# Turning keys and receptances with eight 128-row products into one PSUM bank each in place of sixteen 64-row ones, in a fused RWKV-6 and token-mixing kernel on one Trainium2 core

## The chip, the cores and the metric

The kernel runs on one core of a Trainium2 chip. A core has five engines that run their own instruction streams and wait for each other at semaphores: TensorE (PE) for matrix products, VectorE (DVE), ScalarE (ACT), GpSimd (POOL) and SyncE (SP), which here issues nearly all DMA transfers. Products land in PSUM, an accumulator memory of eight banks of 2 KB per partition, from where VectorE or ScalarE take them to SBUF. The metric is device time in microseconds (us) of one execution; smaller is better.

## The reference, cut to what matters

Inputs are r, k, v and w of shape (4, 8, 768, 48) (batch, heads, sequence, head dimension), u (8, 48), and three matrices. First comes a linear attention with a decaying state, then a token mixer over its output:

```python
for t in range(S):                                   # S = 768
    cur = einsum('bhd,bhe->bhde', u * k[t], v[t])
    y[t] = einsum('bhd,bhde->bhe', r[t], state + cur)
    state = w[t][..., None] * state + einsum('bhd,bhe->bhde', k[t], v[t])
x = y.transpose(0, 2, 1, 3).reshape(B, S, H * D)     # H * D = 384
wq, wk = x @ w_q, x @ w_k                            # 64 columns each
mixed = einsum('bst,btd->bsd', scale * einsum('bsd,btd->bst', wq, wk), x)
out = maximum(mixed, 0) @ w_out
```

## The kernel before

The sequence of each batch is cut into three units of 256 positions (U), so there are 12 units, numbered 0 to 11. A unit is two chunks (c = 0, 1) of 128 positions (C). Within a chunk the recurrence is written as products of decayed keys and receptances, from chunk to chunk goes the state SB. After the third unit of a batch comes the token mixer of that batch.

What happens in a unit, by the names of the steps:

- `wg`, `kg`, `rg`, `vg` are loaded by SP in rings of four buffers, so that the loads can run several units ahead. `ln` takes the logarithm of w to `lw`; `k16`, `r16`, `v16` are casts to bf16, mostly on POOL (k, r, v in the profile).
- `cw` (PS<-CM,lw) sums the logarithms along the positions, in 16 products of 64 rows. ScalarE makes from it the decays `ep` and `en`.
- `kT` and `rT` (PS<-PM,k and PS<-PM,r) turn keys and receptances so that the head dimension lies on the partitions. A cast tensor has the positions of chunk 0 in partitions 0 to 63 and of chunk 1 in 64 to 127 (two per partition, side by side). A turning product takes 64 rows of one chunk as weights (64x128) and the 64x64 corner of the permutation PM as the moving operand. It is done 16 times for a tensor: four pairs of heads, two positions, two chunks.
- Both land in one buffer `kr` of two neighbouring PSUM banks (a "wide" buffer, line 464): chunk 0 in the first bank and chunk 1 in the second, keys in the first half of each bank and receptances in the second half. `turned` (lines 488 to 491) gives the view in which the evictions read it.
- `ks` copies the keys to SBUF; `qT` (receptances times keys, for the bonus u), `RT` (receptances times decay) and `KT` (keys times inverse decay) follow, on VectorE and POOL. Then `A` (PS<-RT,KT, 8 products of 48 rows) for each chunk, its masked eviction `AM`, and `ya` (PS<-VB,AM) and `yi` (PS<-SB,RT, 48 rows), which form y. `kb` turns KT back for the state, `kd` evicts it, `sn` (PS<-SB,IDU and PS<-VB,kd) forms the state and `SB` evicts it. `vp` (PS<-v,PM) sorts the values, `dps` (PS<-UB,qT) makes the bonus.
- The mixer: `X` forms the attention's output, `xt` and `XT` turn it (PS<-ID,X), `qk` projects it, `T`, `mx` (PS<-QK,TS), `fp` (PS<-wo,MX) and `os` end with the store.

All products go through the helper `mm` on line 179, so the profile tells them apart by tiles only. The order of the work is written out by hand: a step is added with what it waits for, and the table ORDER (line 82) lists all steps in the order in which they are issued; each engine gets its own steps in that order and runs them strictly one after the other. WAYS picks the engine of a step that could go to several, BANKS the PSUM banks of a buffer. At the end of the list stand WARM = 12 products of zeros (`z`, PS<-Z), which ORDER spreads over the program; the last of them, step 733, is the last product on TensorE.

The sixteen products for a tensor of the units 1 to 11 (the `long` form, with four positions per partition) are these, lines 470 to 477:

```python
for hp in range(2):
    for s in range(4):
        for c in range(2):
            rows = ds(c * 64, 64)
            x = c * 1024 + place + hp * C + (s % 2) * 64 + (s // 2) * 32
            mm(view(o, x, [[256, 2], [1, 32]]),
               src.tile[rows, ds(s * 256 + hp * 128, 128)],
               PM[rows, rows], trans=True)
```

Of the kernel before, what the change touches and what calls it, by code (L numbers as in the profile page):

```python
# [23 lines left out]
class Buf:  # L24
    def __init__(self, kind, tile=None):
        self.kind = kind
        self.tile = tile
        self.filler = None
        self.before = None
        self.bank = None  # L30


class Plan:
# [89 lines left out]
]  # L123
WAYS = (
    "PDDDAPPDDdPADPPDDEEEAAPPAdPAAPEAcEEAAPPAPPADPeDEEDAAAAAAAAPPDPDADPeAcEEDAPPAdPAAPEAEEEDA"
# [1 line left out]
    "DPPAPeAcceAAPPDPPPAPPAEEDDAEDADAAADAAAADADDA"  # L127
)
BANKS = [
# [6 lines left out]
]  # L136


WARM = 12


@with_exitstack
def kernel(
# [170 lines left out]
    def bank():  # L314
        return Buf("s")
# [66 lines left out]
    def unit(n, batch):  # L382
# [80 lines left out]

        kr = wide()

        def transposed(name, src, step, place):
            def f(e):
                o = at(kr, BF16)
                if long:
                    for hp in range(2):  # L470
                        for s in range(4):
# [6 lines that stand above are left out]
                    return  # L478
                for hp in range(NP):
                    for j in range(2):  # L480
                        for c in range(2):
                            rows = ds(c * 64, 64)
                            mm(o[:, ds(c * 1024 + place + hp * C + j * 64, 64)],
                               src.tile[rows, ds(j * 512 + hp * 128, 128)],
                               PM[rows, rows], trans=True)
            return add((name, n), "E", f, [step], kr, [src], mode=1)

        def turned(place, cs=(0, 1), runs=False):

            return view(at(kr, BF16), place + cs[0] * 1024, [[1024, len(cs)]] * (len(cs) > 1) +  # L490
                        ([[32, 16], [1, 32]] if runs else [[1, 512]]))

        def plain(t, cs=(0, 1), run=0):
# [172 lines left out]
        def of(c, h):  # L666
            return at(ys[c])[:, ds(h * D if end else h % 2 * 512 + (c * NP + h // 2) * D, D)]

        def f_yi(e, c, start):
            heads = [(hp, hh) for hp in range(NP) for hh in range(2)]  # L670
            if end:
                heads.sort(key=lambda x: x[1])
            for x, (hp, hh) in enumerate(heads):
                if end and x == NP:
                    nc.tensor.drain()
                mm(of(c, 2 * hp + hh), RT.tile[ds(hh * 64, D), ds((c * NP + hp) * C, C)],
                   olds[c].tile[ds(hh * 64, D), ds(hp * D, D)],
                   start=(start and hp == 0 and not (end and hh)), stop=False)

        def f_ya(e, c, start):  # L680
            for h in range(H):
                hp, hh = divmod(h, 2)
                mm(of(c, h), AM[c].tile[:, ds(hh * 512 + hp * C, C)],
# [1 line left out]

        def y_add(c):
            yas[c] = add(("ya", n, c), "E",
                         lambda e, c=c, x=ys[c].filler is None: f_ya(e, c, x), [AMs[c], VBs], ys[c],
                         [AM[c], VB])
        for c in range(2):  # L690
            if olds[c] is None:
                y_add(c)
            else:
                yis[c] = add(("yi", n, c), "E",
                             lambda e, c=c, x=ys[c].filler is None: f_yi(e, c, x),
                             [RTs[c], oldss[c]], ys[c], [RT, olds[c]], mode=1)
        for c in range(2):
            if c not in yas:
# [92 lines left out]
        def f_T(e, gs):  # L791
            for gi in gs:
                ii, c = divmod(gi, 2)
                mm(at(T)[ds(c * DH, DH), ds(0, DM)], QK.tile[:, ds(ii * QS + U + c * DH, DH)],
                   X.tile[:, ds(gi * DM, DM)], start=(gi < 2), stop=(gi >= NCH - 2))
        parts = [list(range(4)), [4], [5]] if end else [list(range(NCH))]
        Tp = [add(("T", n, gs[0]), "E", lambda e, gs=gs: f_T(e, gs),
                  [batch["k"][x] for x in gs] + [batch["x"][x] for x in gs], T, [QK, X], mode=2,
# [54 lines left out]
    for n in range(N):  # L853
        if n % NU == 0:
            batch = {"k": [], "q": [], "x": []}
        unit(n, batch)
    for x in range(WARM):
        z = bank()
        add(("z", x), "E", lambda e, z=z: mm(at(z), Z[:, ds(0, C)], Z), [], z, [z])

# [33 lines left out]
```

## Time and profile before

| | |
|---|---|
| median of 3 runs | 101.39 us (101.14 to 102.23) |
| profiled execution | 101.37 us, of which 99.6 us are the span from the first to the last instruction |
| TensorE clock granted | full over the whole span |
| keys turned (PS<-PM,k) | 192 products, 190 ns each by the record, 5.2 us of busy time |
| receptances turned (PS<-PM,r) | 192 products, 190 ns each, 4.9 us of busy time |
| full transposes of X (PS<-ID,X) | 60 products of 128x128, 220 ns each, 5.2 us |
| DMA | 24.68 MB, 248 GB/s over the span |

How to read it: a matmul's record lasts from its start to its modelled end, and several are under way at a time. So 16 products of 190 ns each can take a quarter of a us together, and what a group costs its successor is the distance between their starts. The timeline puts neighbouring instructions of one kind into a row: start, length, engine, line, operation, tiles, rows*columns of the weights, the shape that moves, and the count; in brackets stands how long the engine was idle ahead of it and what released it. "Issue" there means that nothing in the profile explains the wait.

### The profile page before, as it was taken

To read this page: it belongs to the slowest core of one execution; us is meant where nothing else is said; L and a number is where in the kernel's file an instruction comes from. 1 tells how busy PE (TensorE), PEld (TensorE's weight loads), DVE (VectorE), ACT (ScalarE), POOL (GpSimd) and SP (SyncE) were. 2 spreads that over 40 slices of the span, in tenths; PEclk is the share of its full clock that TensorE was granted. 3 is DMA by queue.
4 is the path that set the end of the run, shared out by engine and by line. 5 is a ranking of instruction groups with operands and counts; after the bars stand their busy time and mean duration, and the time that the engine had idled before them with its cause. 6 is when DMAs were issued, how large, how long until landed. Compare 5 with 4: busy or idle time off the path is not lost.

```text
span 99.6 us, 4492 instructions
## 1 busy us (share of the span) xinstructions
PE 86.6 (87%) x1906; PEld 63.3 (64%) x1911; DVE 84.9 (85%) x154; ACT 79.0 (79%) x135; POOL 69.5 (70%) x82
## 2 busy tenths in 40 slices
PE   5978796879886998999999999889998999999930
PEld 1325473756774767777776777759787687776610
DVE  6284999799979999979999999999999799783740
ACT  6034998799996799899999998999899766666920
POOL 6866354999799895799999989498996392500000
PEclk9999999999999999999999999999999999999999
DMA  1999999799999999999999977998993056030794
GB/s 17 313 327 349 324 337 296 195 295 335 289 314 298 225 311 329 344 321 268 271 330 305 316 114 218 251 156 201 282 417 115 7 210 264 10 158 7 277 367 149
DMA packets 45141, 24.68 MB, mean 248 GB/s; under 512 B 31552, under 2 KB 43968, under 8 KB 45120
## 3 DMA queue, kind: packets, MB, share of 16 engines
q1 hardware_dynamic: 44960, 24.19, 84.0%
q8 instruction: 15, 0.25, 0.9%
q10 hardware_dynamic: 160, 0.20, 0.5%
q14 instruction: 6, 0.05, 0.1%
HBM read 19.66 MB, written 4.72 MB: 245 GB/s over the span
## 4 chain that ended last, share of the span: by engine, by line
PE 37%; DVE 23%; SPq 20%; DMA 7%; issue 7%; ACT 3%; ACTq 0%; DVEq 0%
PE PS L179 37%; SPq L232 9%; SPq L237 8%; DMA vg<-in_v_dram 7%; DVE AM L595 7%; DVE X L710 6%; DVE RT L516 3%; SPq L355 2%; DVE qT L506 2%; DVE ks L333 2%; DVE SB L658 1%; ACT VB L327 1%; SPq L357 1%; ACT MX L339 1%; DVE kd L335 1%
## 5 line engine op out<-in xcount | busy, mean ns | idle before, releaser
L595 DVE TENSOR_TENSOR AM<-PS,US 128x1024 bf16<-128x1024 f32 x24 | 28.8, 1218 | 0.7 <-PE PS L179 0.7
L526 POOL TENSOR_TENSOR KT<-ks,en 128x1024 bf16<-128x1024 bf16 (+1 forms) x10 | 19.7, 1965 | 4.7 <-DVE ks L333 3.3
L575 POOL TENSOR_TENSOR Vd<-VB,dd 128x768 bf16<-128x768 bf16 (+1 forms) x14 | 18.1, 1293 | 4.5 <-ACT dd L327 3.4
L454 ACT ACTIVATE en<-PS 128x1024 bf16<-128x1024 f32 (+1 forms) x14 | 12.5, 907 | 3.0 <-PE PS L179 2.9
L179 PEld LDWEIGHTS <-KT 48*128 48x128 bf16 (+1 forms) x312 | 9.7, 94 | 6.6 <-issue 4.5
L447 ACT ACTIVATE ep<-PS 128x512 bf16<-128x512 f32 (+1 forms) x28 | 13.7, 555 | 0.1
L179 PE MATMUL PS<-wo,MX 128*128 128x384 bf16 x72 | 13.5, 327 | 0.0
L710 DVE SCALAR_TENSOR_TENSOR X<-PS,gx,Vd 128x384 bf16<-128x384 f32 x22 | 12.5, 609 | 0.7 <-PE PS L179 0.6
L407 ACT ACTIVATE lw<-wg 128x768 bf16<-128x768 f32 x12 | 10.3, 857 | 2.9 <-DMA wg<-in_w_dram 2.9
L179 PE MATMUL PS<-RT,KT 48*128 48x128 bf16 x192 | 9.7, 218 | 1.2 <-ACT VB L327 0.4
L327 ACT COPY os<-PS 128x768 f32<-128x768 f32 (+1 forms) x11 | 7.9, 714 | 3.5 <-PE PS L179 3.5
L418 POOL CAST k<-kg 128x768 bf16<-128x768 f32 x10 | 8.3, 827 | 2.5 <-DMA kg<-in_k_dram 2.5
L179 PE MATMUL PS<-Z 128*128 128x512 bf16 x25 | 8.4, 461 | 1.4 <-DVE Z L250 1.2
L418 POOL CAST r<-rg 128x768 bf16<-128x768 f32 x10 | 8.2, 825 | 1.6 <-DMA rg<-in_r_dram 1.6
L179 PEld LDWEIGHTS <-MX 128*128 128x128 bf16 x72 | 6.5, 97 | 3.6 <-DVE MX L341 0.2
L516 DVE TENSOR_TENSOR RT<-PS,ep 128x1024 bf16<-128x1024 bf16 (+1 forms) x14 | 8.4, 605 | 0.0
L179 PE MATMUL PS<-VB,AM 128*128 128x48 bf16 x192 | 8.0, 184 | 0.4 <-issue 0.4
L506 DVE TENSOR_TENSOR qT<-PS,ks 128x1024 bf16<-128x1024 bf16 x12 | 8.2, 684 | 0.1
L339 ACT ACTIVATE MX<-PS 128x768 bf16<-128x768 f32 (+1 forms) x12 | 8.0, 682 | 0.4
L179 PE MATMUL PS<-CM,lw 64*128 64x128 bf16 x192 | 7.4, 217 | 0.5 <-DVE AM L595 0.3
L327 ACT CAST VB<-PS 128x768 bf16<-128x768 f32 x8 | 6.4, 804 | 1.1 <-PE PS L179 0.6
L179 PEld LDWEIGHTS <-AM 128*128 128x128 bf16 x192 | 6.3, 96 | 1.6 <-issue 0.7
(90 smaller groups left out, 191.9 us busy)
## 6 DMA issues: line engine op xcount, KB each, us to landing
kg<-in_k_dram SPq DMA_DIRECT2D x12, 384.0 KB, 6.4
wg<-in_w_dram SPq DMA_DIRECT2D x12, 384.0 KB, 5.0
rg<-in_r_dram SPq DMA_DIRECT2D x12, 384.0 KB, 5.8
vg<-in_v_dram SPq DMA_DIRECT2D x9, 384.0 KB, 6.3
out_dram<-os SPq DMA_DIRECT2D x9, 384.0 KB, 2.5
vw<-in_v_dram SPq DMA_DIRECT2D x4, 288.0 KB, 6.7
out_dram<-os SPq DMA_DIRECT2D x5, 192.0 KB, 2.4
wof<-in_moe_w_out_dram SPq DMA_DIRECT2D x1, 576.0 KB, 6.2
```

The lines of the kernel that those rows point to most:

```text
L179: return nc.tensor.matmul(o, l, rr, start=start, stop=stop, skip_group_check=True, is_transpose=trans)
L327: nc.scalar.copy(o, i)
L407: nc.scalar.activation(view(lw.tile, 0, [[64, H], [512, 2], [1, D]]), view(g["wg"].tile, 0, [[D2, H], [D, 2], [1, D]]), ACT.Ln, bias=0.0, ...
L418: op(view(o.tile, 0, [[64, NP], [256, 4], [1, D]]), view(g[src].tile, 0, [[2 * D2, NP], [D, 4], [1, D]]))
L447: nc.scalar.activation(view(ep.tile, cs[0] * NP * EW + off, [[EW, NP * len(cs)], [step, 2], [1, 32]]), view(at(cw), cs[0] * 512 + j * 64, ...
L454: nc.scalar.activation(en.tile[:, ds(cs[0] * 512, w_)], at(cw)[:, ds(cs[0] * 512, w_)], ACT.Exp, bias=0.0, scale=-1.0)
L506: lambda e: nc.vector.tensor_tensor(plain(qT.tile), turned(512), plain(ks.tile), ALU.mult),
L516: nc.vector.tensor_tensor(plain(RT.tile, cs, 32), turned(512, cs, True), plain(ep.tile, cs, EW // 4), ALU.mult)
L526: x.tensor_tensor(KT.tile[:, cols], ks.tile[:, cols], en.tile[:, cols], ALU.mult)
L575: (nc.vector if e == "D" else nc.gpsimd).tensor_tensor(Vd.tile[:, cols], VB.tile[:, cols], view(dd.tile, cs[0] * H, [[1, len(cs) * H], [0, ...
L595: AMs[c] = add(("AM", n, c), "D", lambda e, c=c, A=A: nc.vector.tensor_tensor(view(AM[c].tile, 0, [[C, 8], [1, C]]), view(at(A), 0, [[C, 8 ...
L710: nc.vector.scalar_tensor_tensor(view(X.tile, 2 * i * DM + hh * D, [[D2, H], [1, D]]), view(at(y), hh * 512, [[D, H], [1, D]]), gx, view(V ...
```

## The change

For the units 0 to 10 (`FULL`) a turning product takes the full 128 rows of the cast tensor, both chunks at once, as weights, and the whole permutation PM (128x128) as the moving operand. PM has the two 64x64 corners and zeros elsewhere, so the values are the same. Eight products per tensor take the place of sixteen, each with 128 moving columns where there were 64. Since one product must write to one bank, the layout of `kr` changes too: the keys of both chunks fill the first bank, the receptances the second, and `turned` reads accordingly. Unit 11 stays as it was.

The flags that start an accumulation in `yi`, `ya` and `T` are now set by the first product issued (`begin`), where they had been set by the order in which steps were added. The last of the zero products, step 733, is dropped. ORDER and BANKS lose their entries for it and are otherwise the same numbers in other line breaks; WAYS is unchanged. TensorE's stream goes from 3,824 rows to 3,470: 22 tensors times 8 products with their weight loads (352 rows), and the zero product with its load. No step moves against another on any engine.

```diff
+FULL = tuple(range(11))
...
+        full = n in FULL
+
         def transposed(name, src, step, place):
             def f(e):
                 o = at(kr, BF16)
+                if full:
+                    y = 2 * place
+                    for hp in range(2 if long else NP):
+                        for s in range(4 if long else 2):
+                            if long:
+                                x = view(o, y + hp * C + (s % 2) * 64 + (s // 2) * 32,
+                                         [[512, 2], [256, 2], [1, 32]])
+                            else:
+                                x = view(o, y + hp * C + s * 64, [[512, 2], [1, 64]])
+                            mm(x, src.tile[:, ds(s * (256 if long else 512) + hp * 128, 128)],
+                               PM, trans=True)
+                    return
                 if long:
...
         def turned(place, cs=(0, 1), runs=False):
-
-            return view(at(kr, BF16), place + cs[0] * 1024, [[1024, len(cs)]] * (len(cs) > 1) +
+            w = 512 if full else 1024
+            return view(at(kr, BF16), place * (2 if full else 1) + cs[0] * w,
+                        [[w, len(cs)]] * (len(cs) > 1) +
                         ([[32, 16], [1, 32]] if runs else [[1, 512]]))
...
+    def begin(self, part=None):
+        new = part not in self.begun
+        self.begun.add(part)
+        return new
...
-        def f_yi(e, c, start):
+        def f_yi(e, c):
+            start = ys[c].begin()
...
+                start = T.begin(c)
...
     for x in range(WARM):
+        if x == 11:
+            continue
```

The two forms as they stand in TensorE's stream, at the end of the keys of unit 10 and the start of its `yi`, first before (with the load of its weights ahead of each product, and in brackets what a row waits for):

```order
L179 LDWEIGHTS k_0_89
L179 MATMUL PS<-PM,k_0_89 128x2x32
L179 LDWEIGHTS RT_99
L179 MATMUL PS<-SB_116,RT_99 128x48 [waits Activation_49]
L179 LDWEIGHTS RT_99
```

and after:

```order
L187 LDWEIGHTS k_0_89
L187 MATMUL PS<-PM,k_0_89 128x4x32
L187 LDWEIGHTS RT_99
L187 MATMUL PS<-SB_116,RT_99 128x48 [waits Activation_49]
L187 LDWEIGHTS RT_99
```

The neighbours are the same; a product now writes 4 runs of 32 columns where it wrote 2, and half as many of them stand ahead of `yi`.

More of the change, by code (lines that the diff above doesn't have):

```diff
@@ L30, in __init__ @@
         self.bank = None
+        self.begun = set()
+    def begin(self, part=None):
+        new = part not in self.begun
+        self.begun.add(part)
+        return new
 class Plan:
@@ L678, in f_yi, with f_ya @@
                    start=(start and hp == 0 and not (end and hh)), stop=False)
-        def f_ya(e, c, start):
+        def f_ya(e, c):
+            start = ys[c].begin()
             for h in range(H):
@@ L687, in y_add @@
             yas[c] = add(("ya", n, c), "E",
-                         lambda e, c=c, x=ys[c].filler is None: f_ya(e, c, x), [AMs[c], VBs], ys[c],
+                         lambda e, c=c: f_ya(e, c), [AMs[c], VBs], ys[c],
                          [AM[c], VB])
@@ L694, in unit @@
                 yis[c] = add(("yi", n, c), "E",
-                             lambda e, c=c, x=ys[c].filler is None: f_yi(e, c, x),
+                             lambda e, c=c: f_yi(e, c),
                              [RTs[c], oldss[c]], ys[c], [RT, olds[c]], mode=1)
@@ L793, in f_T @@
                 ii, c = divmod(gi, 2)
+                start = T.begin(c)
                 mm(at(T)[ds(c * DH, DH), ds(0, DM)], QK.tile[:, ds(ii * QS + U + c * DH, DH)],
-                   X.tile[:, ds(gi * DM, DM)], start=(gi < 2), stop=(gi >= NCH - 2))
+                   X.tile[:, ds(gi * DM, DM)], start=start, stop=(gi >= NCH - 2))
         parts = [list(range(4)), [4], [5]] if end else [list(range(NCH))]
```

81 rows, old and new, of tables (BANKS, ORDER) are left out of this document.

## The prediction, made before the changed kernel was timed

> **What bounds the kernel now.** I read the page first, then the busy time by stages, then the chain that ended last, then TensorE's timeline row by row. The page's first row gives each engine's busy time; the table by stages has, for each stretch in us, its length, then the busy time of PE, PEld, DVE, ACT and POOL, the granted clock and the load on the DMA engines.
>
> ```profile
> PE 86.6 (87%) x1906; PEld 63.3 (64%) x1911; DVE 84.9 (85%) x154; ACT 79.0 (79%) x135; POOL 69.5 (70%) x82
> ...
> 0.00:31.00 31.00, 24.74 (x512) 16.39 (x516) 25.14 (x57) 22.96 (x38) 23.11 (x42) 1.00 0.99 283
> 31.00:44.00 13.00, 12.11 (x283) 9.07 (x285) 12.67 (x22) 11.22 (x18) 10.93 (x11) 1.00 1.04 306
> 44.00:67.00 23.00, 21.97 (x582) 16.97 (x577) 22.77 (x37) 22.64 (x38) 21.02 (x20) 1.00 1.00 250
> 67.00:78.00 11.00, 10.33 (x292) 8.69 (x291) 10.07 (x17) 10.49 (x20) 9.09 (x8) 1.00 0.77 235
> ```
>
> No engine is free for long anywhere after 31 us: between 44 and 67 us DVE is busy for 22.77 of 23.00 us and PE for 21.97. An average can't say which of the two is the limit, so I ask the chain (start, length, what):
>
> ```profile
> 21.53 7.07 DMA vg<-in_v_dram
> ...
> 32.23 4.46 PE PS L179 x110
> ...
> 53.14 1.13 DVE AM L595
> ...
> 67.17 9.67 PE PS L179 x260
> ...
> 85.56 10.02 PE PS L179 x107
> ...
> 95.64 0.48 ACT os L327
> ```
>
> So there are four stages. Up to 28.60 us (21.53 + 7.07) the chain is loads. From 32 to 44 us it is TensorE, from there to 67 us VectorE, one piece after another, and from 67.17 us to the last eviction TensorE again. The change touches TensorE alone, so its worth is read from these stages one by one.
>
> **The price of one turned tensor.** TensorE's timeline (start, length, operation, tiles, rows*columns of the weights, shape, count). The starts matter, not the lengths, because matmuls are pipelined:
>
> ```profile
> 46.10 0.41 PE L179 MATMUL PS<-PM,k 64*128 64x64 bf16 x16
> 46.33 0.41 PE L179 MATMUL PS<-PM,r 64*128 64x64 bf16 x16
> 46.68 1.15 PE L179 MATMUL PS<-wo,MX 128*128 128x384 bf16 x6
> ...
> 52.43 0.51 PE L179 MATMUL PS<-ID,X 128*128 128x128 bf16 x6
> 52.77 0.61 PE L179 MATMUL PS<-ID,KT 128*128 128x128 bf16 x8
> 53.31 0.36 PE L179 MATMUL PS<-v,PM 64*64 64x384 bf16 x4
> ```
>
> Sixteen 64-row products take 0.23 us (46.10 to 46.33), 14 ns each: the two halves of the rows run beside each other. Six full transposes, the nearest row to the new form, take 0.34 us (52.43 to 52.77), 57 ns each, so eight take 0.45 us. Halving the count doubles the time: +0.22 us for each of 22 groups (keys and receptances of eleven units), 4.8 us of TensorE work in all. The new output goes out in runs of 32 elements, which the ID rows don't show; the old one does so too in 14 ns, so I add nothing for that. As bounds of one group: 0, if a full product went no slower than the two halves it replaces (not less, since as many elements pass through), and +0.31, with the 0.54 us that eight ID,KT take up to the next group (52.77 to 53.31). I take +0.22, from the row of the same shape with nothing else in it.
>
> The second price is the seam between 64-row and 128-row work. From the receptances at 46.33 to the full product at 46.68 are 0.35 us, 0.12 more than the 0.23 from 46.10; and of those 0.54 us, 0.45 are the eight products' own. A seam costs about 0.1 us. (The Trainium skill, "TensorEngine Tiling (Array Packing)", Key Properties, says that a change of tiling mode drains TensorE; it gives no figure, and the rows here agree with about 0.1 us.) The turned groups change sides, so seams go where their neighbours are full products and come where these have 64 or 48 rows: unit 5, between two full products, loses two; unit 9, between A and the decay sums, gains two; unit 10, where both groups lie between 64- and 48-row ones, gains four. Of the rest unit 0 loses two, unit 1 gains one and unit 4's keys lose one, all ahead of 32 us.
>
> **What can be hidden, stage by stage.** Units 0 to 3 and the keys of unit 4, which come right behind the second row below, lie before 32 us. There the chain is loads, and TensorE waits for others:
>
> ```profile
> 13.76 0.41 PE L179 MATMUL PS<-PM,r 64*128 64x64 bf16 x16 [0.19 <-ACT ks L327]
> ...
> 31.18 0.36 PE L179 MATMUL PS<-v,PM 64*64 64x384 bf16 x4 [0.70 <-DVE RT L516]
> ```
>
> Eight groups (1.8 us) run ahead of that 0.70 us wait, over a stage in which PE is busy for 24.74 of 31 us. I cost them and unit 4's keys at nothing; their cover is the load of v that lands at 28.60. If it were gone, part of 9 x 0.22 = 2.0 us would show.
>
> From 31 to 44 us lie unit 4's receptances and unit 5: 3 x 0.22 = 0.66, less two seams, 0.2: +0.46 us on a TensorE chain. Against it stands a pause, one of four like it. These are waits in the middle of a group, for nothing that the profile names:
>
> ```profile
> 28.75 0.21 PE L179 MATMUL PS<-VB,AM 128*128 128x48 bf16 x2 [0.40 <-issue]
> ...
> 39.77 0.26 PE L179 MATMUL PS<-VB,kd 128*128 128x48 bf16 x4 [0.23 <-issue]
> ...
> 45.97 0.29 PE L179 MATMUL PS<-RT,KT 48*128 48x128 bf16 x4 [0.17 <-issue]
> ...
> 77.34 0.29 PE L179 MATMUL PS<-PM,k 64*128 64x64 bf16 x8 [0.51 <-issue]
> ...
> q8 instruction: 15, 0.25, 0.9%
> ```
>
> Counted along TensorE's order, they follow rows 958, 1470, 1726 and 3262: all apart by multiples of 256. The instruction queue moved 15 packets, and 3,824 rows over 15 are 255. So the pauses are TensorE running out of fetched instructions, and they come where rows are used up fast; 32 rows of sixteen small products go by in 0.23 us, faster than nearly anything else. The change takes 354 rows (22 x 16 + 2), puts the boundaries elsewhere, and uses 16 rows in 0.45 us where it used 32 in 0.23. I count the pauses at 39.77, 45.97 and 77.34 as gone: -0.23, -0.17, -0.51 = -0.91 us in all; the one at 28.75 is covered as above. Bounds: 0, if they only move, and -0.91. (The Trainium skill, "Runtime: NRT & Kernel Launch", Instruction fetch mechanics, has fetches in blocks of 256 instructions, which agrees, and their cost mostly hidden, which these rows don't bear out: four of 15 show. By that sentence there would be nothing to gain here, and the sum would be higher by the 0.91.) This stage then comes to +0.46 - 0.23 = +0.2 us, which one wait for data can take up; I take +0.1.
>
> From 44 to 67 us lie units 6 to 9: 8 x 0.22 + 2 seams = 2.0 us. VectorE is the chain here, so only what TensorE can't make up shows. Where it had time to spare is seen from starts that lie further apart than the same work needs:
>
> ```profile
> 49.46 0.62 PE L179 MATMUL PS<-CM,lw 64*128 64x128 bf16 x16
> 49.92 0.40 PE L179 MATMUL PS<-PM,k 64*128 64x64 bf16 x16
> ...
> 55.32 0.62 PE L179 MATMUL PS<-CM,lw 64*128 64x128 bf16 x16
> 55.98 0.41 PE L179 MATMUL PS<-PM,k 64*128 64x64 bf16 x16
> ...
> 58.66 0.34 PE L179 MATMUL PS<-UB,qT 128*128 128x2 bf16 x8
> 59.16 0.24 PE L179 MATMUL PS<-SB,IDU 128*128 128x192 bf16 x1 [0.16 <-ACT ep L447]
> ...
> 62.60 0.37 PE L179 MATMUL PS<-VB,AM 128*128 128x48 bf16 x8
> 63.17 0.24 PE L179 MATMUL PS<-SB,IDU 128*128 128x192 bf16 x1 [0.19 <-DVE AM L595]
> ...
> 66.35 0.62 PE L179 MATMUL PS<-CM,lw 64*128 64x128 bf16 x16
> ```
>
> The decay sums need 0.46 us (49.46 to 49.92); they had 0.66 from 55.32, and 0.82 from 66.35 to the next group at 67.17: 0.20 and 0.36 to spare. Eight small full products need about 0.2 us; those at 58.66 had 0.50 and those at 62.60 had 0.57: 0.30 and 0.37. With the pause at 45.97 (0.17) that is 1.4 us, and 2.0 - 1.4 leaves +0.6 us. It shows at evictions that are fed just in time, as here (a row of TensorE's timeline, then one of VectorE's):
>
> ```profile
> 50.69 0.50 PE L179 MATMUL PS<-ID,X 128*128 128x128 bf16 x6
> ...
> 51.40 0.55 DVE L333 COPY XT<-PS 128x768 bf16<-128x768 bf16 x1
> ```
>
> The transposes stand behind unit 7's turned groups and end at 51.19, 0.21 us ahead of the copy; 0.44 us later they end 0.23 us behind its start. What is late next is every VectorE step after it. Bounds: 0 and 2.0.
>
> From 67.17 us on TensorE is the chain, and unit 10 stands at its head:
>
> ```profile
> 67.17 0.41 PE L179 MATMUL PS<-PM,k 64*128 64x64 bf16 x16 [0.19 <-DVE AM L595]
> 67.39 0.28 PE L179 MATMUL PS<-SB,RT 48*128 48x48 bf16 x8
> 67.50 0.41 PE L179 MATMUL PS<-PM,r 64*128 64x64 bf16 x16
> 67.73 0.28 PE L179 MATMUL PS<-SB,RT 48*128 48x48 bf16 x8
> 67.94 0.73 PE L179 MATMUL PS<-VB,AM 128*128 128x48 bf16 x16
> ```
>
> 2 x 0.22, and three of the four new seams, since the first falls into the 0.19 us wait: +0.74 us. The sixteen products at 67.94 take 0.73 us in which they wait for AM; some 0.2 us of delay vanish there. The pause at 77.34 gives back 0.51. Remainder: +0.03, rounded to nothing; bounds 0 - 0.2 and +0.74.
>
> At no cost: the new starting flags change no instruction. The zero product that goes is TensorE's last instruction, behind the product that releases the eviction at 95.64, and nothing waits for it. With keys and receptances in a bank each, the receptance products needn't wait for the copy of the keys any more; of this the rows show one wait, 0.19 us at 13.76 us, inside the loads. VectorE's and ScalarE's reads keep their sizes.
>
> Sum: 0 + 0.1 + 0.6 + 0 = +0.7 us. The profiled execution took 101.37 us (99.6 us of span and 1.8 around it); the median of three runs is 101.39, the same to a few hundredths, so nothing has to be carried over. I forecast 102.1.
>
> **The rivals.** *TensorE limits everything from 31 us on.* Nothing is made up and pauses only move: 13 groups x 0.22 + 4 seams net (minus two, plus two, plus four) x 0.1 = +3.3, 104.7 us. For it: PE busy for 21.97 of 23 us. Against it: the gaps above.
>
> *The pauses stay.* Fetches are as late as before, at other places. All else as in the sum: 0.7 + 0.9, 102.9 us. For it: where the boundaries fall is chance; against it: rows are used up more slowly.
>
> *Faster: the pauses decide.* The pauses go, and the added work of all stages hides, in gaps of TensorE that its busy time covers up: 101.4 - 0.9 = 100.5 us. It decides from the point where VectorE between 44 and 67 us never waits for a product, and unit 10's 0.74 us are made up before the last third. For it: VectorE sets that stage, and its inputs mostly stand ready half a us early. Against it: unit 10 lies on TensorE's own chain.
>
> *It does nothing that can be seen,* because the full transposes run in the shadow of what TensorE waits for and the pauses move too: 101.4 us; it lies within the forecast's own range.
>
> **How the numbers follow.** The forecast, with the case of nothing to be seen: 0.47 (101.2 to 102.7). Pauses stay: 0.17. TensorE limits everything, in whole or in most: 0.15 (103.3 to 104.7). Faster: 0.21 (99.9 to 101.2). The range from 100.4 to 103.5 leaves out about 0.1 at either end. About 1% is what a measurement of this kernel can tell from no change, so the borders are 100.4 and 102.4. Faster by more: the lower half of its case, 0.13, and a little for what I don't see: 0.16. Slower by more: 0.15 + 0.14 of the pauses' case, and 0.08 of the forecast's upper end: 0.37. Within: 0.47.
>
> **What would show it.** In the profile after: eight products for a group, and 0.45 us from its start to the next start of full products; seams of 0.1 us on both sides of unit 10's groups; PE's busy time up by about 4 us; instruction packets down to 14 or 13, and no pauses in the middle of groups in the last 60 us. VectorE should wait for PE a few tenths between 50 and 60 us. The forecast is wrong if a group takes 0.3 us or less, if mid-group pauses total as much as before, or if the start of unit 10's keys moves from 67.17 by more than 2 us.

## The result, and the profile after

Over 22 runs of each, the changed kernel took a median of 102.34 us (101.72 to 104.39) and the kernel before 101.73 us (100.19 to 105.83); the ratio is 1.0134, with a 95% interval of 1.0103 to 1.0165. It is slower by a little over 1%, near the forecast of 102.1 us. (The ratios leave out the executions that took over 1.5% longer than the quickest of their kernel, here about half of the kernel before's 22 and two of the changed kernel's, which is why this one is larger than the ratio of the two medians, 1.006; of e1_shift56 only one execution was left, so it has no ratio, and the profiled executions of e3, e6, e7 and e8 had a granted clock of 0.76 to 0.90 in some stretches of ten us before 40 us, so they are read only where it was full.)

The page of the kernel after, busy time and instruction packets, then the table by stages, with the columns of before:

```profile
PE 90.1 (90%) x1730; PEld 66.9 (67%) x1734; DVE 85.3 (85%) x154; ACT 79.1 (79%) x135; POOL 70.2 (70%) x82
...
q8 instruction: 13, 0.21, 1.0%
```

```profile
31.00:44.00 13.00, 12.61 (x282) 9.89 (x281) 12.57 (x21) 11.81 (x20) 10.56 (x10) 1.00 1.00 292
44.00:67.00 23.00, 22.23 (x472) 17.32 (x472) 22.15 (x36) 21.81 (x35) 20.13 (x19) 1.00 1.09 248
67.00:78.00 11.00, 10.86 (x282) 9.12 (x276) 10.24 (x17) 10.01 (x19) 9.33 (x8) 1.00 0.79 233
```

PE's busy time grew by 3.5 us. Between 44 and 67 us the two busiest engines changed places: VectorE had 22.77 us and TensorE 21.97, now TensorE has 22.23 and VectorE 22.15. The chain of waits says the same; there the long pieces from 30 us on are TensorE's, where it had been VectorE's evictions one after another:

```profile
30.11 5.68 PE PS L187 x121
...
45.05 2.04 PE PS L187 x22
...
48.72 3.15 PE PS L187 x52
...
55.00 2.41 PE PS L187 x50
...
59.57 4.24 PE PS L187 x100
...
67.29 16.18 PE PS L187 x382
...
95.65 0.48 ACT os L335
```

The last eviction starts at 95.65 us, against 95.64 before: in the two profiled executions (101.72 and 101.37 us) the change seems to cost nothing up to there. That is the sum of gains and losses. From the starts of the keys' groups in TensorE's timelines, in us:

| stretch | before | after | difference | predicted |
|---|---|---|---|---|
| span's start to unit 4's keys | 31.47 | 30.39 | -1.08 | 0 |
| unit 4's keys to unit 6's | 14.63 | 14.66 | +0.03 | -0.1 |
| unit 6's keys to unit 10's | 21.07 | 22.24 | +1.17 | +0.8 |
| unit 10's keys to the last eviction | 28.47 | 28.36 | -0.11 | 0 |
| last eviction to the end of the span | 3.97 | 4.36 | +0.39 | 0 |

(The forecast had counted the pause at 45.97, 0.17 us, with the third row; here it stands where it lies, in the second.) And the profiled execution of the kernel after was the quickest of its 22, while the one of before was not: the ratio holds about 1 us more than this pair shows.

TensorE's timeline of the kernel after, at unit 6, at unit 10, and at unit 11's old-form groups, where the pause of 0.51 us had been:

```profile
45.05 0.61 PE L187 MATMUL PS<-PM,k 128*128 128x128 bf16 x8 [0.18 <-ACT kd L337]
45.50 0.61 PE L187 MATMUL PS<-PM,r 128*128 128x128 bf16 x8
45.94 1.14 PE L187 MATMUL PS<-wo,MX 128*128 128x384 bf16 x6
...
67.29 0.61 PE L187 MATMUL PS<-PM,k 128*128 128x128 bf16 x8
67.83 0.27 PE L187 MATMUL PS<-SB,RT 48*128 48x48 bf16 x8
68.04 0.62 PE L187 MATMUL PS<-PM,r 128*128 128x128 bf16 x8
68.59 0.27 PE L187 MATMUL PS<-SB,RT 48*128 48x48 bf16 x8
68.79 0.57 PE L187 MATMUL PS<-VB,AM 128*128 128x48 bf16 x16
69.21 0.49 PE L187 MATMUL PS<-ID,X 128*128 128x128 bf16 x6
...
77.24 0.41 PE L187 MATMUL PS<-PM,k 64*128 64x64 bf16 x16
77.48 0.40 PE L187 MATMUL PS<-PM,r 64*128 64x64 bf16 x16
```

A group takes 0.45 and 0.44 us. At unit 10 each group takes 0.54 or 0.55, and the eight 48-row products between the two groups take 0.21 where they took 0.11: about a tenth of a us at every new seam. (Those behind the second group stand ahead of full products in both kernels and take 0.20 and 0.21.) VectorE, just in time before, now waits for the transposes behind unit 7's groups:

```profile
50.98 0.56 DVE L341 COPY XT<-PS 128x768 bf16<-128x768 bf16 x1 [0.36 <-PE PS L187]
```

What the forecast hadn't counted on is at the start. The kernel before: the load of the keys of unit 2 (KB, us from issue to landing) and the instruction packets moved between 11 and 14.5 us; then POOL's cast of these keys:

```profile
kg<-in_k_dram SPq DMA_DIRECT2D x1, 384.0 KB, 7.1
...
q8 instruction: 1, 0.02, 2.0%
```

```profile
16.64 0.82 POOL L418 CAST k<-kg 128x768 bf16<-128x768 f32 x1 [1.47 <-DMA kg<-in_k_dram]
```

The same load in the kernel after, with the packet now between 14.5 and 17 us, and the cast:

```profile
kg<-in_k_dram SPq DMA_DIRECT2D x1, 384.0 KB, 5.7
...
q8 instruction: 1, 0.02, 2.9%
```

```profile
15.31 0.82 POOL L426 CAST k<-kg 128x768 bf16<-128x768 f32 x1
```

The load lands 1.4 us sooner after its issue, the cast waits for nothing, and unit 2's keys start at 16.96 us in place of 17.52. So at unit 2's keys half a us is gained, at a place where the forecast had nothing. Whether it lasts up to unit 4's keys, where the first row of the table ends, is taken up with e9 and e10.

### The profile page after: what moved, and what is told of

Same layout as the page of the kernel before. It is cut to its first block, busy times and chain, and to the rows that moved or that the text cites. A ratio compares the mean times of both kernels' runs of the same rounds, so it can differ in the third digit from the quotient of the medians.

```text
span 100.0 us, 4138 instructions
## 1 busy us (share of the span) xinstructions
PE 90.1 (90%) x1730; PEld 66.9 (67%) x1734; DVE 85.3 (85%) x154; ACT 79.1 (79%) x135; POOL 70.2 (70%) x82
## 4 chain that ended last, share of the span: by engine, by line
PE 60%; ACT 13%; DVE 13%; issue 7%; POOL 3%; DVEq 0%; POOLq 0%; ACTq 0%
PE PS L187 60%; DVE X L735 3%; ACT ep L455 3%; DVE AM L618 2%; ACT en L462 2%; DVE RT L539 2%; ACT lw L415 2%; ACT kd L337 2%; DVE SB L681 2%; ACT os L335 1%; ACT VB L335 1%; DVE kd L306 1%; POOL US L294 1%; POOL CM L276 1%; DVE qT L529 1%
## 5 line engine op out<-in xcount | busy, mean ns | idle before, releaser
L187 PE MATMUL PS<-PM,k 128*128 128x128 bf16 (+1 forms) x104 | 7.2, 215 | 0.3 <-ACT kd L337 0.2
L681 DVE TENSOR_TENSOR SB<-PS,ep 128x192 bf16<-128x192 f32 x20 | 7.0, 351 | 0.3 <-PE PS L187 0.3
```

Of the source, the lines that this page charges most:

```text
L187: return nc.tensor.matmul(o, l, rr, start=start, stop=stop, skip_group_check=True, is_transpose=trans)
```

## The experiments

Twelve experiments ran, in three comparisons with the kernel before of five rounds each; its medians there were 102.24, 101.85 and 101.67 us. e5 is the changed kernel as it stands, and e9 is e6 again. The others but e1 and e2 are the changed kernel with one line edited, the list of units that have the new form (e10 has a second edit, shown below):

```diff
-FULL = tuple(range(11))
+FULL = (6, 7, 8, 9)
```

**Which units cost what.** The old form in all units, which leaves of the change the starting flags and the dropped product:

> The changed kernel with no unit in the new form: only the starting flags and the dropped last zero product are left of the change. Every theory: time of before (ratio 1.000, at most 0.3% off), pauses at the rows 958, 1470, 1726 and 3262 as before. If it is off by 0.5% or more, the rest of the change has a cost or a gain that the prediction left out.

It took 101.71 us, ratio 0.9958 (0.9907 to 1.0009). What the forecast had put at no cost shows no cost. The part on the pauses came out half: they stand after rows 958 (0.21 us) and 3262 (0.25), none over 0.15 us after 1470 and 1726, and one that the kernel before didn't have, after row 2494:

```profile
61.54 0.29 PE L187 MATMUL PS<-PM,r 64*128 64x64 bf16 x8 [0.47 <-issue]
```

But for its last product this kernel issues the same rows as the kernel before, so the pauses differ from one execution to the next.

All units but unit 10:

> The changed kernel with units 0 to 9 in the new form and unit 10 in the old one. Theory P (products and seams of unit 10 lie on TensorE's own chain from 67 us on, 0.74 us, and show in full): 0.7 us less than the changed kernel, 0.99 of it, as long as no pause comes back behind 67 us. Rival H (they are taken up by waits behind them, such as the one of the products at 67.94 for AM): 0 to 0.2 us less.

101.85 us, ratio 0.9986 (0.9947 to 1.0025): without unit 10 the change can't be told from nothing. That is 1.2 to 1.5% under the whole change (ratios 1.0105 and 1.0134), more than the 0.7 us of theory P; rival H doesn't fit.

Unit 10 alone:

> Only unit 10 in the new form. Theory P (0.74 us of products and seams on TensorE's own chain): from unit 10's keys to unit 11's 9.9 us (9.4 to 9.6 in the old form), and from unit 10's keys to the last product 28.3 with no pause at unit 11's keys, or 28.9 with one; time + 0.6 us less what the lost pause gives back, ratio 1.000 to 1.006. Rival H: from unit 10's keys to unit 11's 9.6 us or less, nothing to be seen.

103.38 us, ratio 1.0177 (1.0112 to 1.0242). Its profiled execution shows the price of unit 10 as in the kernel after: 28.36 us from its keys (68.50) to the last eviction (96.86). The old form without a pause takes 27.79 in e9 (67.43 to 95.22) and 28.02 in e2 (68.26 to 96.28), so unit 10 costs 0.3 to 0.6 us there. From its keys to unit 11's are 9.94 us, as theory P had it. The ratio is larger than the forecast's 1.000 to 1.006. Two pauses of 1.05 and 0.55 us stand in this execution at 29 and 41 us, ahead of anything that the edit touches, and the granted clock was 0.83 between 10 and 20 us and 0.85 between 30 and 40; whether the other runs have these pauses too, the times can't say. Why e3 and e8 both put unit 10 higher than this stretch does stays open.

Units 6 to 9 alone:

> Only units 6 to 9 in the new form, 2.0 us more work on TensorE by the prediction, of which it let 0.6 show. Theory S (what the traces show of the changed kernel holds by itself: unit 6 to 7 +0.40, 7 to 8 +0.24, 8 to 9 +0.40, 9 to 10 +0.1): from unit 6 to unit 10 22.2 us where the old form has 21.1, and a time 1.1 us above that of before, ratio 1.010, plus or minus a pause. Rival (the way is longer in the changed kernel only because it comes there 1 us earlier, ahead of its loads): 21.1 to 21.5 us, ratio 1.000 to 1.003.

102.65 us, ratio 1.0082 (1.0031 to 1.0133). From unit 6's keys to unit 10's it takes 22.24 us, as the kernel after (22.24) and its repetition (22.23), against 21.07 before. The stage costs 1.2 us wherever the rest stands.

The whole change again:

> The changed kernel once more, beside the kernel before on one chip. By the starts of the keys' groups in the traces so far: the way from unit 6 to unit 10 takes 22.2 us (21.1 to 21.2 in the kernels with the old form and no pause there), from unit 10 to the last product 28.3 (28.15 to 28.4 in the old form). Theory E (the changed kernel's early start in its first trace, unit 4's keys at 30.39 us where the old form has 30.85 to 31.47, is the change's own): unit 4's keys at 30.4 again, time of before + 0.4 us, ratio 1.004. Theory N (it was chance of the loads): unit 4's keys near 31.2, time of before + 1.2 us, ratio 1.012.

102.75 us, ratio 1.0105 (1.0047 to 1.0163), in line with the first. Unit 4's keys start at 30.70 us, between the two theories; the ratio is near theory N's 1.012, and theory E's 1.004 lies outside the interval. So the early start of the first trace is at most in part the change's own. Its profiled execution took 102.30 us; the last store takes 3.0 us to land there as in the kernel after, where the kernel before and e4 had 2.3 and 2.4:

```profile
out_dram<-os ACTq DMA_DIRECT2D x1, 192.0 KB, 3.0
```

That is most of the 0.39 us in the table's last row. Why the store takes longer wasn't tried.

Units 0 to 3 alone:

> Only units 0 to 3 in the new form. Prediction's step (they are hidden behind the loads and cost nothing): unit 4's keys at 31.2 us, every later stretch as in the old form but for pauses at other places (128 rows fewer put boundaries near unit 9 and unit 10), ratio 0.995 to 1.005. Theory E: unit 4's keys at 30.4, ratio 0.990 to 0.997. A cost that the prediction missed: unit 4's keys after 31.6, ratio above 1.005.

100.63 us, ratio 0.9883 (0.9818 to 0.9948): quicker than both kernels, and below what any of the three theories had. (In the profiled execution unit 4's keys start at 31.63 us, but its granted clock was 0.83 between 30 and 40.) That was a surprise, and it went into the third comparison, again as it was:

> The new form in units 0 to 3 alone, as in e6_full_0_3 (100.63 us, ratio 0.988). If that gain is real it comes again: unit 2's keys start at 16.9 to 17.0 us where they start at 17.4 to 17.5 with the old form, unit 3's at 25.9 (26.3 to 26.4), the ratio is 0.985 to 0.995. If e6's runs were only lucky in where instruction blocks arrive late, the ratio is 0.998 or more.

100.65 us, ratio 0.9896 (0.9825 to 0.9967). The gain came again, and this is the best version found. In both, unit 2's keys start at 16.95 us.

**Where the early gain comes from.** The new form uses fewer rows, so an instruction packet that had been fetched at 13 us is fetched later. To part this from the products themselves, e10 has e9's products but puts 64 rows back in front, in about the same time:

```diff
-        for _ in range(18):
+        for _ in range(14):
             mm(PS[:, ds(0, 512)], Z[:, ds(0, C)], Z)
+        for _ in range(36):
+            mm(PS[:, ds(0, 8)], Z[:, ds(0, C)], Z[:, ds(0, 8)])
```

> The new form in units 0 to 3, and ahead of everything 14 zero products of 512 columns and 36 of 8 columns in place of 18 of 512 columns: 64 rows more in about the same time, as many as units 0 and 1 save ahead of unit 2's keys. The products, the waits and the data are those of e9. Theory F (the gain comes from one instruction block being fetched at 15 us and not at 13, so that it doesn't hold up the load of keys for unit 2): the fetch moves back to 12.8 to 13.3 us, POOL's cast of the keys for unit 2 waits over 1 us for the load again and starts at 16.4 to 16.7, unit 2's keys start at 17.4 to 17.5. Theory W (it comes from the new form itself, whose receptance products don't wait for the copy of the keys): the cast starts at 15.2 to 15.4 and unit 2's keys at 16.9 to 17.0, wherever the fetch falls.

101.09 us, ratio 1.0010 (0.9965 to 1.0054): no gain. e9's load, packet (14.5 to 17 us) and cast:

```profile
kg<-in_k_dram SPq DMA_DIRECT2D x1, 384.0 KB, 5.7
...
q8 instruction: 1, 0.02, 2.8%
```

```profile
15.30 0.82 POOL L426 CAST k<-kg 128x768 bf16<-128x768 f32 x1
```

and e10's, with its packet between 11 and 14.5 us:

```profile
kg<-in_k_dram SPq DMA_DIRECT2D x1, 384.0 KB, 6.5
...
q8 instruction: 1, 0.02, 2.0%
```

```profile
16.48 0.82 POOL L428 CAST k<-kg 128x768 bf16<-128x768 f32 x1 [1.01 <-PE PS L187]
```

The cast moved back by 1.2 us and unit 2's keys to 17.36, close to theory F's 17.4; theory W, which had the cast at 15.2 to 15.4, falls. (Of the 0.41 us at unit 2's keys 0.19 stand already at unit 0's and unit 1's. The wait's label names TensorE, but the load had only just landed: it was issued at 9.83, 0.34 later than in e9, and landed 6.5 later, at 16.3.)

In the profiled executions of seven kernels the packet came between 11 and 14.5 us (before, e1, e4, e7, e8, e10, e12), and the load took 6.5 to 7.2 us; in five it came later (after, e5, e6, e9, e11), and the load took 5.7 in each. e2, whose packet came at 9.24, has 6.9. But e3, whose products are those of the kernel after up to there, has the late packet (15.20) and a load of 8.1 us, at a clock that was full up to 18 us. So a late packet goes with a quick load but doesn't ensure it, and something else can hold the load up too. The packet's share, 2.0% of 16 engines over 3.5 us, is 1.1 us of one DMA engine. That it holds up that engine's part of the load is an inference.

Nor does the gain at unit 2's keys reach unit 4's keys. TensorE's row there, first in e9 and then in e10:

```profile
30.84 0.41 PE L187 MATMUL PS<-PM,k 64*128 64x64 bf16 x16
```

```profile
30.75 0.41 PE L187 MATMUL PS<-PM,k 64*128 64x64 bf16 x16
```

e4, with the old form, has them at 30.85. Ahead of them stands VectorE's cast of v, which took 1.72 us from 27.59 in e9 and 1.42 from 27.79 in e10. The last eviction starts at 95.22 in e9, with a pause of 1.17 us on the way, and at 94.97 in e10, with two of 0.34 and 0.40. So these two executions don't show that the early load makes e9 the quicker kernel. The 64 rows move every later block boundary too, and with them the places of the pauses: that e6 and e9 gain by the places of their boundaries is a rival that no run here tests, since both have the same ones.

Units 0 and 1, and units 2 and 3, apart:

> The new form in units 0 and 1 alone. Theories F and W both have unit 2's keys at 16.9 to 17.0 us here, since these two units save 64 rows and have no wait for the copy of the keys; unit 3's keys then start at 25.9 and the ratio is 0.985 to 0.995, the same as with units 0 to 3. If units 2 and 3 bring a part of the gain, unit 3's keys start at 26.1 or later and the ratio is above that of e9.

> The new form in units 2 and 3 alone; rows and waits ahead of unit 2's keys are those of the kernel before. F and W: unit 2's keys start at 17.4 to 17.6 us, POOL's cast of its keys waits over 1 us for the load, and the ratio is 0.995 to 1.005. If the full products gain by themselves in units 2 and 3, unit 4's keys start 0.3 us or more earlier, counted from unit 2's, than in the kernel before (13.79 us) and the ratio is under 0.995.

e11 took 101.67 us, ratio 1.0049 (1.0005 to 1.0092); e12 101.31 us, 0.9973 (0.9934 to 1.0011). e12 is near what was expected (cast at 16.42, unit 2's keys at 17.30). From there to unit 4's keys it takes 13.40 us, but so does the old form in e4 (13.41), so the full products gain nothing by themselves. e11 has the quick load (5.7 us), yet no gain: its whole start lies 0.57 us later (unit 0's keys at 8.51 us in place of 7.94), so unit 2's keys start at 17.43, and then it pauses in the middle of a group:

```profile
18.77 0.27 PE L187 MATMUL PS<-VB,AM 128*128 128x48 bf16 x4
19.32 0.26 PE L187 MATMUL PS<-VB,AM 128*128 128x48 bf16 x4 [0.27 <-issue]
```

So the quick load alone doesn't decide; the later start, which wasn't looked into, and the pause take it back. The expectation, that units 0 and 1 bring it all, failed.

**The pauses.** Two kernels from before's file move the boundaries without touching the turned groups: 56 rows more (e1), with 32 small zero products in place of four large ones, and 160 rows more (e2), with 91 in place of eleven, as in the diff of e10:

> The kernel before with 56 more rows ahead of the first unit on TensorE (the last 4 of the 18 zero products of 512 columns at the start give way to 32 of 8 columns); all else as before. Theory F (the mid-group pauses are late instruction blocks of 256 rows): the block boundaries now fall on stretches of the program in which the last 140 rows ahead of them took 2.5 us or more, so the pauses at 39.77, 45.97 and 77.34 us are gone and the time falls by 0.91 us, to about 100.5 (ratio 0.991). Rival G (the pauses belong to the places in the work, or to the DMA load there): they stay where they are, ratio 1.000.

> The kernel before with 160 more rows ahead of the first unit (11 of the 18 zero products give way to 91 of 8 columns). Theory F: the boundaries fall on other fast stretches, and pauses stand near 58, 63, 68 and 74 us, those at 63 and 68 of about 0.5 us or more each; the two at 68 and 74 lie on TensorE's chain, so the time is that of before or up to 0.5 us more (ratio 1.000 to 1.005), and 1 us or more above the variant with 56 rows. Rival G: pauses at 39.8, 46.0 and 77.3 as before, ratio 1.000.

The one run of e1 that is left took 100.85 us, too little to judge the time. Two rows of its TensorE timeline on either side of a boundary, and a third further on:

```profile
32.95 0.25 PE L179 MATMUL PS<-PM,r 64*128 64x64 bf16 x6
33.40 0.32 PE L179 MATMUL PS<-PM,r 64*128 64x64 bf16 x10 [0.20 <-issue]
...
66.42 0.40 PE L179 MATMUL PS<-RT,KT 48*128 48x128 bf16 x8 [0.43 <-issue]
```

They follow rows 1214 and 2750 of TensorE's order. At the four products where the kernel before paused there is no pause, though these products are the same. The rows 958, 1470, 1726 and 3262 there and these two all leave 190 when divided by 256. So the pauses hang on the count of rows, as the forecast had it, and rival G falls. That the new places would bring none was wrong. e2 took 101.59 us, ratio 0.9961 (0.9916 to 1.0006), and shows no such pause at all, where some had been expected. (Its time says little of pauses: its products up to 16 us are slower, 0.61 us for a group that lasts 0.41 in the kernel before, and unit 4's keys start at 32.75 in place of 31.47.)

The packets' own times in the traces tell why some boundaries bring a pause and others don't. Behind 18 us TensorE crosses 179 boundaries in the fourteen profiled executions, and 22 of them bring a pause over 0.15 us. At all 22 TensorE got there no later than 1.25 us after the end of the last packet, and went on 1.27 to 1.67 us after that end, however long it had stood. Of the other 157 it reached all but two 1.29 us or more after that end (the two at 1.02 and 1.08), in e2 all of them 1.38 us or more. So a pause is TensorE waiting for a packet that came late, as the forecast had said.

The same product at the same row paused in e11 and e12 for different times, first e11, then e12:

```profile
41.64 0.49 PE L187 MATMUL PS<-XT,wq 128*128 128x256 bf16 x3 [0.67 <-issue]
...
47.01 0.23 PE L187 MATMUL PS<-PM,r 64*128 64x64 bf16 x4 [0.28 <-issue]
```

```profile
41.63 0.49 PE L187 MATMUL PS<-XT,wq 128*128 128x256 bf16 x3 [0.96 <-issue]
...
47.55 0.23 PE L187 MATMUL PS<-PM,r 64*128 64x64 bf16 x4 [0.82 <-issue]
```

Their rows are 1470 and 1726, as in the kernel before, which paused there for 0.23 and 0.17 us. A pause belongs to an execution as much as to a kernel.

## Why the prediction was right, and where it wasn't

**The price of a group: right.** 0.45 us was forecast, and 0.45 and 0.44 were measured. **The seams: right.** At unit 10 the AM products start 0.85 us later than before (68.79 against 67.94) after keys that start 0.12 later: +0.73, forecast +0.74.

**Up to 32 us, "at no cost": right as to the cost.** The eight groups cost nothing, as said. But the step took their cover, the loads, as a fixed thing. The forecast had moved the block boundaries by the rows saved and priced that on TensorE alone, while the profile counts the packets to the same 16 DMA engines as the loads; with a later packet went a quicker load and a gain of about 0.5 us at unit 2's keys (16.96 against 17.52). At unit 4's keys, where the stage ends, little is left of it that could be called the change's: the changed kernel has 30.39 and 30.70, e9 30.84, and the old form 30.85 (e4) to 31.47 (before). The other half of the 1.08 us lies between unit 3's and unit 4's keys (4.51 us against 5.05) and is no part of the change, since e4, with the old form, takes 4.51 too; in the kernel before VectorE waits 0.73 us for a load of v there.

**From unit 4 to unit 6: right.** +0.03 us, where the pause had been counted as gone. Without a pause the old form takes 14.33 us here (e9, 30.84 to 45.17), so the products cost 0.32: the +0.46 less part of a wait, as forecast. The repetition takes 14.91 us (30.70 to 45.61), which is 0.58, on the other side of the 0.46.

**From unit 6 to unit 10: a term mis-sized.** +1.17 us where the terms gave +0.8 (2.0 of work less 1.23 of TensorE slack). The step that failed is the slack, "0.20 and 0.36 to spare" of the decay sums and "0.30 and 0.37" of the small products. TensorE's timeline after, at these places:

```profile
55.00 0.62 PE L187 MATMUL PS<-CM,lw 64*128 64x128 bf16 x16
55.57 0.61 PE L187 MATMUL PS<-PM,k 128*128 128x128 bf16 x8
...
58.55 0.34 PE L187 MATMUL PS<-UB,qT 128*128 128x2 bf16 x8
59.05 0.24 PE L187 MATMUL PS<-SB,IDU 128*128 128x192 bf16 x1 [0.16 <-ACT ep L455]
...
63.14 0.37 PE L187 MATMUL PS<-VB,AM 128*128 128x48 bf16 x8
63.35 0.24 PE L187 MATMUL PS<-SB,IDU 128*128 128x192 bf16 x1
...
66.54 0.62 PE L187 MATMUL PS<-CM,lw 64*128 64x128 bf16 x16
```

At 63.14 the wait for AM is used up, 0.57 us having become 0.21. At 58.55 none of the slack was used: it is 0.50 us before and after. The decay sums gave 0.09 (0.57 us from 55.00 to 55.57, was 0.66) and 0.07 (0.75 from 66.54 to 67.29, was 0.82). Of 1.23 us 0.52 were used; the stage found some 0.3 elsewhere. Why 58.55 gave nothing is seen on ScalarE, first before, then after:

```profile
57.22 0.90 ACT L329 ACTIVATE kd<-PS,gk 128x768 bf16<-128x768 bf16 x1
58.02 1.09 ACT L447 ACTIVATE ep<-PS 128x512 bf16<-128x512 f32 x2
```

```profile
57.11 0.90 ACT L337 ACTIVATE kd<-PS,gk 128x768 bf16<-128x768 bf16 x1
57.91 1.09 ACT L455 ACTIVATE ep<-PS 128x512 bf16<-128x512 f32 x2
```

The product waits for `ep`, which stands on ScalarE right behind `kd`, and `kd` evicts the ID,KT products that TensorE issues straight after unit 8's turned groups (56.46 to 57.00 us after, 56.56 to 57.11 before). From unit 8's keys to `kd` it was 1.24 us and is now 1.54: the wait moves with the work that was to fill it. That reading of the rows is argued; no run took `ep` from behind `kd`.

**From unit 10 on: right.** -0.11 us in the profiled pair, since the pause there is gone. Without a pause the products cost 0.3 to 0.6 us (28.36 against 28.02 and 27.79); +0.74 - 0.2 had been forecast. (The wait for AM gave 0.16: from 67.94 to 68.52 it was 0.58 us, from 68.79 to 69.21 it is 0.42.)

**The pauses: right in cause; their size rested on one execution.** In the kernel after and its repetition there are none over 0.15 us after 31 us, as forecast. But the 0.91 us were taken from one execution of before and set against the median, "so nothing has to be carried over". The two times agreed; what they were made of need not: e4, with the same rows but for the last product, lost 0.72 us behind 31 us, in part at another boundary. Without pauses the products cost 0.32 to 0.58, 1.17 and 0.3 to 0.6 us, the last store 0.4, less 0 to 0.5 at the start: +1.7 to +2.8. The ratio's 1.3% then leaves 0.3 to 1.4 us that the runs of before lose to pauses on the average, an estimate, which can't tell whether 0.91 was too much. (The Trainium skill, "Runtime: NRT & Kernel Launch", Instruction fetch mechanics, has the cost of a block boundary mostly hidden; e2 agrees, the 0.96 and 0.82 us of e12 don't.)

So it is partly luck that 102.1 came out near 102.34: the stage from unit 6 to unit 10 was put too low by 0.4 us, the last store's 0.4 wasn't in the sum, and what stood against them, the start and the pauses, isn't fixed by these runs to better than half a us.

**The rivals.** TensorE limits everything (104.7): it is on the chain nearly everywhere now, but 0.52 us of slack was there, and the time stayed far below. The pauses stay (102.9): the time alone wouldn't decide against it, but the two profiles have no pause over 0.15 us. Nothing that can be seen (101.4): the interval of the ratio leaves out 1. Faster (100.5): not for the whole change; kernels with the new form in units 0 to 3 alone came near that time (100.63 and 100.65), but there the added work lies under the loads, and the profiled execution of e9 still paused for 1.17 us, so this isn't the rival's mechanism.

## What to carry to other kernels

A wait that a product spends on another engine may not be slack if the other engine is itself waiting for products behind the same edit; follow the releaser back two or three steps before counting it. A change in the number of instructions moves the fetches too, and here a late load went with an early fetch: look at both when a kernel gets quicker or slower at a place that wasn't touched, and follow a gain to the end of the stage before counting it. Pauses of one profiled execution are not a property of the kernel; take them out on both sides of a sum. And put a change of form only into those stages whose cover was seen to hold.

## What was not expected of the hardware

A packet of 0.02 MB between 11 and 14.5 us goes with a 384 KB load that takes 6.5 to 7.2 us in place of 5.7 (seven executions against five; in e3 the load took 8.1 us with a later packet). From 18 us on, and where the clock was full, TensorE's pauses that nothing in the profile explains, those over 0.15 us, stand only after rows that leave 190 when divided by 256, last 0.16 to 1.2 us (1.17 in e9), and differ between executions of the same rows. They end 1.27 to 1.67 us after the end of an instruction packet. The last store of 192 KB landed in 3.0 us in both profiled executions of the whole change and in 2.3 before; the cause is open.
